# A fused attention and FFN kernel: the second FFN in seven block products instead of eight from the third batch on

## The chip, the cores and the metric

The kernel runs on one core of a Trainium2 chip. The core has a matrix engine (TensorE, PE in the profile, with PEld for its weight loads), VectorE (DVE), ScalarE (ACT), GpSimd (POOL) and SyncE (SP), which here only starts DMA transfers. Matmul results go to PSUM, which has eight banks of 128 partitions by 512 float32. All other tiles lie in SBUF. The engines run side by side and wait for each other through semaphores. The metric is the device time of one execution in microseconds; lower is better.

## What is computed

```python
def _attn_ref(q, k, v, phi):                    # 8 batches, 8 heads, 576 rows, 64 wide; phi has 32 memories
    a = np.exp(phi - np.max(phi, axis=2, keepdims=True))
    a = a / (np.sum(a, axis=2, keepdims=True) + 1e-09)
    k_m = np.einsum('bhsm,bhsd->bhmd', a, k)
    v_m = np.einsum('bhsm,bhsd->bhmd', a, v)
    scores = np.matmul(q, k_m.transpose(0, 1, 3, 2)) / np.sqrt(q.shape[-1])
    attn = np.exp(scores - np.max(scores, axis=-1, keepdims=True))
    attn = attn / (np.sum(attn, axis=-1, keepdims=True) + 1e-09)
    return np.matmul(attn, v_m)

def _moe_ref(x, w_in, w_out):                   # x: 4608 tokens x 512; w_in 512 x 2048; w_out 2048 x 512
    h = x @ w_in
    g = h * (1.0 / (1.0 + np.exp(-h)))
    return g @ w_out
```

The attention output, heads side by side, is the `x` of the FFN.

## The kernel before

**Layout.** Work goes by batch (576 tokens). The attention of batch n = b+1 is computed while the FFN of batch b runs. `v_m` and `w_in` are multiplied first (`p_mm`, "P"), so that the first FFN takes the attention weights (`a`, 256 memories of all heads) straight to h. Operands of the big matmuls are split into a high and a low float32r part (`hi`, `lo`), and a product is three matmuls: hi with hi, hi with lo, lo with hi.

**The chunk loop.** A batch has 16 chunks of 128 FFN columns (`fc`, L886). For each chunk `ffn1` (L622) issues 12 matmuls of 288 columns into the tile `h` (two PSUM banks, one buffer); `silu` (L657) on ScalarE writes 512 tokens to `g32` (two buffers) and the other 64 tokens to `gleft`; `split` (L646) on VectorE makes the two parts in `gparts`. `finish` (L874) then issues the previous chunk's second FFN: `main_step` (L689) has four token tiles of 128, each with three matmuls of 512 output columns (`ffn2`, L671) into one of four PSUM banks, "acc". So TensorE's order is FFN1 of chunk c, work of the attention, FFN2 of chunk c-1. After the last chunk `store` (L680) copies each bank with ScalarE and sends it out. After every second batch the 64 leftover tokens of two batches go through `left_step` (L695): four times `split`, then 12 matmuls.

**The events.** `events` (L703 to L756) lists, by batch and chunk slot, the pieces of the next batch's attention: `phi_max`, `phi_fold` (a maximum over partitions), `phi_sub`, `phi_exp`, `e_mm` (k_m and v_m), `e_tr`, `s_all` (scores), `s_max`, `s_sub`, `s_exp`, `s_sum`, `s_norm`, `s_back` and `s_low` (transposes back and parts), and four `p_mm` with their split `p_split`. They run after `ffn1` and the SiLU of the slot. `load_kv`, `load_q` and `load_phi` are also events; they are issued on SP's queue.

**What sets the order.** TensorE follows the written order everywhere (`in_order`, L97), ScalarE from batch 1 on. VectorE and SP are put in order by the compiler's planner: it takes, at each time of its own estimate, the instruction that is ready and stands first in the program. On the chip each engine's list is then fixed. A tile with a `tag` shares its buffers with other tiles of that tag and waits for a free one; `mt` of `phi_max` shares the tag "g32" with the SiLU output (L245, L658). The tag "raw" (three buffers of 8 KB a partition) holds raw weights in batch 0 and output tiles later; "cva" and "cva1" serve the weight conversion of batch 0. `beside_h` (L208) gives unused columns of the h banks, `banks` (L202) the two "bg" banks that P uses.

Of the kernel before, what the change touches and what calls it, by code (L numbers as in the profile page):

```python
# [48 lines left out]
def attn_ffn_kernel(  # L49
# [12 lines left out]
    ps = ctx.enter_context(tc.tile_pool(name="ps", bufs=1, space=bass.MemoryType.PSUM))  # L62

# [11 lines left out]
    pparts = const.tile([P, 2, 2, 2 * JW], F32R, name="pparts")  # L75

# [271 lines left out]
    def e_tr(b):  # L348
        pt = beside_h(P)
        t = sb.tile([P, 2, NR, M], F32, tag="kvT", name=f"kvT{b}", bufs=2)  # L350
        for kind in range(2):
            nc.tensor.transpose(pt[kind], kvn[:, kind].rearrange("p g d -> p (g d)"), ident)  # L352
        nc.vector.tensor_copy(t[:, 0].rearrange("p r m -> p (r m)"), pt[0])
        nc.scalar.copy(t[:, 1].rearrange("p r m -> p (r m)"), pt[1])
# [76 lines left out]
    def set_parts(b):  # L431
        for k, x in enumerate(("ahi", "alo")):
            at[b][x] = aparts[:, k, b % 2].rearrange("p (g s) -> p g s", g=2)

    def s_back(b, u):
        if "aT" not in at[b]:
            at[b]["aT"] = sb.tile([P, 2, S], F32, tag="att", name=f"aT{b}")
            set_parts(b)
        aT, ahi, sc = (at[b][k] for k in ("aT", "ahi", "sc"))
        c = slice(*u)  # L440
        for p in range(2):
            nc.vector.transpose(aT[:, p, c], sc[:, p, c])  # L442
        nc.scalar.activation(ahi[:, :, c], aT[:, :, c], AF.Copy)
# [142 lines left out]
    ALL = (0, S)  # L586
# [3 lines left out]
    pj = {}  # L590

    def p_mm(b, f, w, low=True):
        j = f // JW
        if f % JW == 0:
            pj[b, j] = [pparts[:, k, j % 2].rearrange("p (g f) -> p g f", g=2) for k in range(2)]
# [60 lines left out]

    def silu(b, fc, h):  # L657
        g32 = sb.tile([P, MAIN], F32, tag="g32", name="g32", bufs=2)  # L658
# [10 lines left out]
    acc = {}  # L669
# [10 lines left out]
    def store(key, rows, last=False):  # L680
        o = sb.tile([P, DMODEL], F32, tag="raw", name="o", bufs=RAWB)
# [20 lines left out]

    events = {}  # L703
# [4 lines left out]
    for b in range(B):  # L708
# [4 lines left out]
        else:  # L713
            for j in range(1, NJ):
                ev(b, 4 * j - 3, p_mm, b, j * JW, JW)
        if n == B:
            continue
        at_slot = (4, 5, 6, 7.5, 9, 9.5, 11.5, 12.5, 13, 13.5, 13.5, 14) if b == 0 else (1, 2, 3, 5, 9, 10, 10, 11, 12, 13, 13, 14)
# [27 lines left out]
        ev(b, sk, s_back, n, ALL)  # L746
        ev(b, sk, s_low, n, ALL)
        if n + 1 < B:
            ev(b, sk, load_phi, n + 1)
        ev(b, 14, p_mm, n, 0, JW)  # L750
# [220 lines left out]
```

## Time and profile before

| | |
|---|---|
| time, median of 3 runs | 701.71 us (701.3 to 702.42) |
| span of the profiled execution | 700.3 us; the page gives no separate time for that execution |
| instructions | 11773, of them 4924 matmuls |
| FFN1, 128 x 288 (L637) | 1524 recorded, mean 295 ns |
| FFN2, 128 x 512 (L676, acc) | 1024 with wo_hi, 395 ns; 512 with wo_lo, 392 ns |
| FFN2 of leftover tokens (L676, accleft) | 192 |
| DMA | 60.15 MB, mean 86 GB/s |

The page gives busy time by engine, the span in 40 slices, the DMA queues, the chain of work that ended last, and the costliest groups of instructions. A matmul's duration in it contains its way through the array, and matmuls overlap; their pace is read from the starts in the timeline. A timeline row has start, duration, engine, line, operation, output <- inputs, size and count; in brackets stands the engine's idle time before it and what ended that. A window row has for each engine the busy time and the count of instructions, then the granted TensorE clock, the DMA share and GB/s. A DMA row has the count, KB of each and the median time from issue to landing.

### The profile page before, as it was taken

To read this page: it belongs to the slowest core of one execution; us is meant where nothing else is said; L and a number is where in the kernel's file an instruction comes from. 1 tells how busy PE (TensorE), PEld (TensorE's weight loads), DVE (VectorE), ACT (ScalarE), POOL (GpSimd) and SP (SyncE) were. 2 spreads that over 40 slices of the span, in tenths; PEclk is the share of its full clock that TensorE was granted. 3 is DMA by queue.
4 is the path that set the end of the run, shared out by engine and by line. 5 is a ranking of instruction groups with operands and counts; after the bars stand their busy time and mean duration, and the time that the engine had idled before them with its cause. 6 is when DMAs were issued, how large, how long until landed. Compare 5 with 4: busy or idle time off the path is not lost.

```text
span 700.3 us, 11773 instructions
## 1 busy us (share of the span) xinstructions
PE 689.4 (98%) x4924; PEld 562.4 (80%) x4924; DVE 365.4 (52%) x665; ACT 259.0 (37%) x456; POOL 0.7 (0%) x6
## 2 busy tenths in 40 slices
PE   7999999999999999999999999999999999999997
PEld 3578777888888888888888888888888888888886
DVE  4898797435654256534636346542564525623322
ACT  3879584422424224421423314342241413431211
POOL 0000000000000000000000000000000000000000
PEclk9999999999999999999999999999999999999999
DMA  9995752212201221132110311112121000010002
GB/s 334 317 338 187 254 212 95 78 61 68 92 19 46 92 68 44 52 137 69 35 61 16 137 56 47 61 54 83 68 80 31 1 1 1 1 61 1 1 0 76
DMA packets 25445, 60.15 MB, mean 86 GB/s; under 512 B 2096, under 2 KB 10416, under 8 KB 25392
## 3 DMA queue, kind: packets, MB, share of 16 engines
q1 hardware_dynamic: 24448, 56.63, 22.8%
q10 hardware_dynamic: 944, 2.77, 1.1%
q8 instruction: 39, 0.64, 0.4%
q14 instruction: 14, 0.11, 0.1%
HBM read 49.95 MB, written 9.44 MB: 85 GB/s over the span
## 4 chain that ended last, share of the span: by engine, by line
PE 84%; DVE 2%; issue 0%; ACT 0%; ACTq 0%
PE acc L676 45%; PE h L637 25%; PE accleft L676 6%; PE bg L602 4%; PE h L322 2%; PE bg L367 1%; DVE wo_lo L176 0%; DVE raw L172 0%; PE h L330 0%; PE h L352 0%; DVE aparts L448 0%; DVE aT L442 0%; DVE gparts L654 0%; DVE sc L415 0%; DVE smx L411 0%
## 5 line engine op out<-in xcount | busy, mean ns | idle before, releaser
L676 PE MATMUL acc<-wo_hi,gparts 128*128 128x512 f32 x1024 | 341.8, 395 | 0.1
L676 PEld LDWEIGHTS acc<-wo_hi,gparts 128*128 128x128 f32 x1024 | 192.0, 188 | 52.7 <-issue 6.6
L637 PEld LDWEIGHTS h<-aparts,pparts 128*128 128x128 f32 x1524 | 214.0, 188 | 14.4 <-issue 2.1
L637 PE MATMUL h<-aparts,pparts 128*128 128x288 f32 x1524 | 223.3, 295 | 0.7 <-ACT aparts L581 0.4
L660 ACT ACTIVATE g<-h 128x512 f32<-128x512 f32 x127 | 76.0, 599 | 345.9 <-PE h L637 180.3
L676 PE MATMUL acc<-wo_lo,gparts 128*128 128x512 f32 x512 | 200.8, 392 | 0.7 <-DVE wo_lo L176 0.6
L652 DVE CAST gparts<-g 128x512 fp32r<-128x512 f32 x128 | 54.4, 425 | 260.0 <-ACT g L660 260.0
L676 PEld LDWEIGHTS acc<-wo_lo,gparts 128*128 128x128 f32 x512 | 96.1, 188 | 18.4 <-DVE wo_lo L176 1.9
L654 DVE TENSOR_TENSOR gparts<-g,gparts 128x512 fp32r<-128x512 f32 x128 | 88.2, 689 | 10.3
L618 DVE TENSOR_TENSOR pparts<-bg,pparts 128x1024 fp32r<-128x1024 f32 (+1 forms) x36 | 39.7, 1102 | 5.4 <-ACT pparts L616 5.0
L676 PE MATMUL accleft<-wo_hi,gparts 128*128 128x512 f32 x128 | 40.6, 389 | 0.0
L616 ACT ACTIVATE pparts<-bg 128x1024 fp32r<-128x1024 f32 (+1 forms) x36 | 33.6, 932 | 14.8 <-PE bg L602 14.8
L602 PE MATMUL bg<-win,kvT 64*32 64x512 f32 (+1 forms) x576 | 35.8, 554 | 0.0
L676 PEld LDWEIGHTS accleft<-wo_hi,gparts 128*128 128x128 f32 x128 | 24.0, 188 | 4.9
L662 ACT ACTIVATE gleft<-h 128x64 f32<-128x64 f32 x127 | 27.8, 219 | 0.0
L683 ACT ACTIVATE o<-acc 128x512 f32<-128x512 f32 x32 | 19.2, 600 | 21.8 <-PE acc L676 10.6
L676 PE MATMUL accleft<-wo_lo,gparts 128*128 128x512 f32 x64 | 24.9, 389 | 0.0
L660 ACT ACT_TABLE_LOAD x14 | 18.0, 1283 | 14.2 <-issue 13.6
L652 DVE CAST gparts<-gleft 128x512 fp32r<-128x512 f32 x16 | 6.8, 427 | 20.7 <-PE accleft L676 12.2
L168 ACT ACTIVATE raw<-raw 128x1024 int32<-128x1024 uint32 (+1 forms) x16 | 16.8, 1048 | 0.0
L322 PEld LDWEIGHTS h<-kv,phi 128*32 128x32 f32 x384 | 10.2, 110 | 5.0 <-ACT gleft L662 5.0
L676 PEld LDWEIGHTS accleft<-wo_lo,gparts 128*128 128x128 f32 x64 | 12.0, 188 | 2.4
(139 smaller groups left out, 365.0 us busy)
## 6 DMA issues: line engine op xcount, KB each, us to landing
kv<-in_kv SPq DMA_DIRECT2D x28, 516.0 KB, 5.9
q<-in_q SPq DMA_DIRECT2D x16, 576.0 KB, 5.7
out<-o SPq DMA_DIRECT2D x32, 256.0 KB, 2.1
raw<-in_w_in SPq DMA_DIRECT2D x14, 512.0 KB, 6.6
raw<-in_w_out SPq DMA_DIRECT2D x6, 1024.0 KB, 5.5
phi<-in_phi SPq DMA_DIRECT2D x7, 576.0 KB, 3.8
kv<-in_kv ACTq DMA_DIRECT2D x4, 516.0 KB, 6.8
kr<-in_kv SPq DMA_DIRECT2D x7, 258.0 KB, 6.4
```

What stands on the lines that cost most here:

```text
L168: nc.scalar.activation(r, low, AF.Copy, scale=2.0**-29)
L322: nc.tensor.matmul(pt[p][M * r : M * (r + 1), :KVW], e[:, p, c, M * r : M * (r + 1)], kvt[c][:, p, r], start=c == 0, stop=False, skip_grou ...
L602: nc.tensor.matmul(bg[M * r : M * (r + 1), p, :w].rearrange("p (k f) -> p k f", f=P), kvT[D * p : D * (p + 1), 1, r], win[D * p : D * (p + ...
L616: nc.scalar.activation(hi[:, :, c], bg[:, :, :w], AF.Copy)
L618: nc.vector.tensor_tensor(lo[:, :, c], bg[:, :, :w], hi[:, :, c], op=ALU.subtract)
L637: nc.tensor.matmul(h[:, hf, :HALF], wt[:, p, fs], a[:, p, hf * HALF : (hf + 1) * HALF], start=n[hf] == 0, stop=n[hf] == 5, skip_group_chec ...
L652: nc.vector.tensor_copy(ghi, g32)
L654: last_split.append(nc.vector.tensor_tensor(glo, g32, ghi, op=ALU.subtract))
L660: nc.scalar.activation(g32.rearrange("p (h f) -> p h f", h=2), h[:, :, :w], AF.Silu)
L662: i = nc.scalar.activation(gleft[:, fc, o : o + LEFT].rearrange("p (h f) -> p h f", h=2), h[:, :, w:HALF], AF.Silu)
L676: nc.tensor.matmul(acc[key], gt[:, cs], wt[:, fc], start=fc == 0 and n == 0, stop=fc == NFC - 1 and n == 2)
L683: nc.scalar.activation(o, a, AF.Copy)
```

## The change

Batches 0 and 1 keep the old second FFN. From batch 2 on, the product g @ w_out of 256 tokens, 256 FFN columns and 512 outputs is taken as 2 x 2 blocks of 128 tokens, 128 FFN columns and 256 outputs, and formed from seven block products (Winograd's form of Strassen's method) instead of eight. Each product is again three matmuls, now of 256 columns.

A batch has 16 steps: two token halves (`t`) of eight pairs of chunks (`j`). `ffn1s` makes h of two chunks for 288 tokens (12 matmuls of 288). `forms` applies SiLU and makes the sums of g's blocks and their two parts on VectorE and ScalarE. `st_step` issues 7 x 3 matmuls. Four products use weights that stay in SBUF (three blocks of w_out, and one sum that `t1_load` writes over the fourth block after batch 1), three use weight sums that come from DRAM: `ring_load` fetches 256 KB for each use into a ring of four slots. The seven sums are collected in four PSUM banks, half a bank each; `st_out` combines them after each half and sends out two tiles of 128 tokens.

The weight sums are formed during batch 1 (`w_forms`: GpSimd, ScalarE, VectorE) and stored to DRAM. The leftover tokens of batches 2 to 7 go through `left_st`, with matmuls of 256 columns. All four quarters of P now have to last through a whole batch (two in tag "raw", two in `pparts`), so P and the attention move to other slots, the attention parts have one home from batch 2 on, and the second half of batch n's attention parts (`SECOND`, n from 3) is formed at slot 1 of batch n itself. `mt` moves to tag "cva1", the SiLU output to a fixed buffer `gbuf`. `e_mm` and `e_tr` use the "bg" banks in later batches.

```diff
+    gbuf = const.tile([P, 2 * MAIN], F32, name="gbuf")
...
-            at[b]["mt"] = sb.tile([P, 2, 2, P], F32, tag="g32", name="mt", bufs=2)
+            at[b]["mt"] = sb.tile([P, 2, 2, P], F32, tag="cva1", name="mt", bufs=1)
...
-        pt = banks(b) if b < 2 else beside_h(KVW)
+        pt = beside_h(KVW) if b == 2 else banks(b)
...
-            at[b][x] = aparts[:, k, b % 2].rearrange("p (g s) -> p g s", g=2)
+            at[b][x] = aparts[:, k, b == 1].rearrange("p (g s) -> p g s", g=2)
...
+    def w_forms(j, step):
...
+        if step == 0:
+            f = at[0]["forms", j] = sb.tile([P, 2, DMODEL], F32, tag="cva", name="wf", bufs=1)
+            c = slice(2 * j, 2 * j + 2)
+            nc.gpsimd.tensor_tensor(f, as_f32(wo_hi[:, c]), as_f32(wo_lo[:, c]), op=ALU.add)
+            b11, b12, b21, b22 = (f[:, k, q * Q : (q + 1) * Q] for k in range(2) for q in range(2))
+            nc.gpsimd.tensor_tensor(b11, b12, b11, op=ALU.subtract)
+            nc.gpsimd.tensor_tensor(b12, b22, b12, op=ALU.add)
+            nc.gpsimd.tensor_tensor(b22, b22, b11, op=ALU.add)
+            nc.gpsimd.tensor_tensor(b21, b22, b21, op=ALU.subtract)
+            return
+        f = at[0]["forms", j].rearrange("p k (q f) -> p (k q) f", q=2)
+        nc.scalar.activation(ring[0][:, :, :Q], f, AF.Copy)
+        nc.vector.tensor_tensor(ring[0][:, :, Q:], f, ring[0][:, :, :Q], op=ALU.subtract)
+        load(saved[j], as_f32(ring[0]))
+
+    def t1_load(n):
+        for j in (2 * n, 2 * n + 1):
+            for w, q in ((wo_hi, 0), (wo_lo, Q)):
+                load(as_f32(w[:, 2 * j, Q:]), saved[j][:, 0, q : q + Q])
+
+    RING = (3, 1, 2)
+    uses = [(j, k) for b in range(2, B) for t in range(2) for j in range(NP) for k in RING]
...
+    def ring_load():
+        u = next(asked, None)
+        if u is not None:
+            j, k = uses[u]
+            load(as_f32(ring[0][:, u % 4]), saved[j][:, k])
...
+    def forms(b, t, j, h):
...
+        nc.scalar.activation(gbuf[:, :MAIN].rearrange("p (i f) -> p i f", i=2), h[:, :, :w], AF.Silu)
+        o = b % 2 * LEFT + t * (LEFT // 2)
+        nc.scalar.activation(gleft[:, 2 * j : 2 * j + 2, o : o + LEFT // 2], h[:, :, w:HALF], AF.Silu)
+        hi, lo = form_high[j % 2], form_low[j % 2]
+        nc.scalar.activation(hi[:, :3], g[:, 1:4], AF.Copy)
+        nc.vector.tensor_tensor(
+            g[:, 4:6], g[:, :1].broadcast_to([P, 2, P]), g[:, 1:3], op=ALU.subtract
+        )
+        nc.vector.tensor_tensor(g[:, 6], g[:, 1], g[:, 5], op=ALU.subtract)
+        nc.vector.tensor_tensor(g[:, 7], g[:, 3], g[:, 6], op=ALU.subtract)
+        nc.vector.tensor_copy(hi[:, 3:], g[:, 4:])
+        nc.vector.tensor_tensor(lo, g[:, 1:], hi, op=ALU.subtract)
+        return hi, lo
...
+    def st_step(b, t, j, part):
...
+        held = ((0, 0, 0, b11), (0, 1, 2, b21), (1, 0, 6, b22), (1, 1, 4, b12))
+        for terms in (HIGH, LOW):
+            for bank, place, k, w in held:
+                product(bank, place, part, k, w, terms)
+        for bank, place, k in ((2, 0, 5), (2, 1, 3), (3, 0, 1)):
+            r = ring[0][:, next(used) % 4]
+            product(bank, place, part, k, (r[:, :Q], r[:, Q:]), HIGH + LOW)
+            ring_load()
+        if j == NP - 1:
+            st_out(b, t)
+
+    def st_out(b, t):
...
+        for i in range(2):
+            nc.scalar.activation(o[:, i], sums[i], AF.Copy)
...
+        add(u2, sums[2][:, :Q], c11)
+        add(u3, sums[2][:, Q:], u2)
+        add(c11, c11, c12)
+        add(c12, u2, c22)
+        add(c12, c12, c21)
+        add(c21, u3, sums[3][:, :Q], ALU.subtract)
+        add(c22, u3, c22)
...
+            for j in range(NP):
+                ev(b, 1.5 * j + 2, w_forms, j, 0)
+                ev(b, 1.5 * j + 3, w_forms, j, 1)
+        else:
+            ev(b, 0, p_mm, b, (3 if b > 2 else 2) * JW, JW)
+            if b == 2:
+                ev(b, 2, p_mm, b, 3 * JW, JW)
+            else:
+                ev(b, 1, s_high, b, SECOND)
+                ev(b, 1, s_low, b, SECOND)
...
-        at_slot = (4, 5, 6, 7.5, 9, 9.5, 11.5, 12.5, 13, 13.5, 13.5, 14) if b == 0 else (1, 2, 3, 5, 9, 10, 10, 11, 12, 13, 13, 14)
+        at_slot = (
+            (4, 5, 6, 7.5, 9, 9.5, 11.5, 12.5, 13, 13.5, 13.5, 14) if b == 0
+            else (1, 2, 3, 5, 9, 10, 10, 11, 12, 13, 13, 14) if b == 1
+            else (0, 1, 3, 5, 6, 7, 7, 9, 10, 11, 11, 13)
+        )
...
+            for j in range(3):
+                ev(b, 10 + 2 * j, p_mm, n, j * JW, JW)
...
+        for s in range(NFC if b > 1 else 0):
...
+            t, j = divmod(s, NP)
+            h = ffn1s(b, t, j)
+            part = forms(b, t, j, h)
+            for part_ in range(2):
+                for fn, a in events.pop((b, s + part_ / 2), []):
+                    fn(*a)
+            finish(range(NI))
+            prev = ("st", b, t, j, part)
```

The numbers of `at_slot` are the slots of `phi_max`, the fold, `phi_exp`, `e_mm`, `e_tr`, the scores (twice), `s_max` and `s_sub`, `s_exp`, `s_sum`, `s_norm` and `s_back`.

More of the change, by code (lines that the diff above doesn't have):

```diff
@@ L594, in p_mm @@
         if f % JW == 0:
-            pj[b, j] = [pparts[:, k, j % 2].rearrange("p (g f) -> p g f", g=2) for k in range(2)]
+            p_home(b, j)
         hi, lo = pj[b, j]
@@ L655, in split @@
         return gs
+    half = iter(range(1 << 30))
     def silu(b, fc, h):
-        g32 = sb.tile([P, MAIN], F32, tag="g32", name="g32", bufs=2)
+        g32 = gbuf.rearrange("p (n f) -> p n f", n=2)[:, next(half) % 2]
         w = MAIN // 2
@@ new lines, in product @@
+    def product(bank, place, part, k, w, first):
+        hi, lo = part
+        whi, wlo = w
+        for gt, wt in first:
+            gt, wt = (hi, lo)[gt], (whi, wlo)[wt]
+            key = bank, place
+            nc.tensor.matmul(
+                sums[bank][:, place * Q : (place + 1) * Q], gt[:, k], wt,
+                start=bank not in begun, stop=True, skip_group_check=True,
+            )
+            begun.add(bank)
+    sums, begun = [], set()
+    HIGH, LOW = ((0, 0), (0, 1)), ((1, 0),)
```

155 lines of the change are left out of this document (132 added, 23 removed).

## The prediction

> **What bounds the kernel now.** I began with the page: span, engine table, granted clock.
>
> ```profile
> span 700.3 us, 11773 instructions
> PE 689.4 (98%) x4924; PEld 562.4 (80%) x4924; DVE 365.4 (52%) x665; ACT 259.0 (37%) x456; POOL 0.7 (0%) x6
> ...
> PEclk9999999999999999999999999999999999999999
> ```
>
> TensorE is busy for 689 of 700.3 us at full clock, VectorE for half of it. The next view is PE's timeline over one chunk of 128 FFN columns in the fourth batch: twelve FFN1 matmuls, twelve FFN2 matmuls, the next twelve FFN1.
>
> ```profile
> 403.92 1.75 PE L637 MATMUL h<-aparts,pparts 128*128 128x288 f32 x12
> 405.51 0.39 PE L676 MATMUL acc<-wo_hi,gparts 128*128 128x512 f32 x1
> ...
> 408.25 1.74 PE L637 MATMUL h<-aparts,pparts 128*128 128x288 f32 x12
> ```
>
> The starts give 1.59 us for FFN1 (132 ns a matmul of 288 columns) and 2.74 us for FFN2 (228 ns a matmul of 512), with no gap: a chunk takes 4.33 us and TensorE alone sets it. Next I asked what VectorE does in 85 us of this, about one batch (the phi loads of three successive batches start 77.96 and 88.84 us apart, 83.4 on average; every second batch is followed by the leftover stage).
>
> ```profile
> 225.00:310.00 85.00, 85.00 (x639) 70.76 (x630) 42.00 (x83) 27.96 (x52) 0.00 (x0) 1.00 0.26 90
> ...
> 267.96 0.33 SPq L87 DMA_DIRECT2D phi<-in_phi  x1
> ...
> 345.92 0.33 SPq L87 DMA_DIRECT2D phi<-in_phi  x1
> ...
> 434.76 0.33 SPq L87 DMA_DIRECT2D phi<-in_phi  x1
> ```
>
> PE 85.00, VectorE 42.00, ScalarE 27.96, DMA share 0.26. So a cut in matmul time is worth its full length until VectorE or the DMA queue takes over, and the change loads both.
>
> **TensorE's part.** Per step (two chunks, half the tokens), 21 matmuls of 256 columns replace 12 of 512, in 16 steps a batch and six batches: 96 steps. FFN1's matmuls stay 12 a step. No matmul of this type with 256 columns is in the trace. A line through the two pitches, 228 at 512 and 132.5 at 288, rises 0.426 ns a column and gives 119 ns at 256. Below it, proportion alone (228 / 2) gives 114. Above it, 132.5 would hold if each weight load set a floor that 288 columns already touch. A row with a 128 x 128 load before every matmul of 128 columns speaks against that floor:
>
> ```profile
> 54.91 0.60 PE L265 MATMUL bg<-ident,cm 128*128 128x128 f32 x4
> ...
> L265 PE MATMUL bg<-ident,cm 128*128 128x128 f32 x4 | 0.6, 274 | 0.0
> ```
>
> Four start within 0.60 - 0.27 = 0.33 us, 110 ns apart: a load fits in 110. I take 119. A step is then 1.59 + 21 x 0.119 = 4.09 us, 0.24 less; over 96 steps **-23.0 us** (114 ns: -33; 132.5: +4). The leftover stage of batches 3, 5 and 7 has 96 matmuls of 256 instead of 48 of 512: 11.42 against 10.94 us, **+1.4** for three.
>
> **VectorE's chain.** A chunk's split was a cast and a subtraction; a step now needs a subtraction over 256 elements, two over 128, a cast of 512 and a subtraction over 896.
>
> ```profile
> L652 DVE CAST gparts<-g 128x512 fp32r<-128x512 f32 x128 | 54.4, 425 | 260.0 <-ACT g L660 260.0
> L654 DVE TENSOR_TENSOR gparts<-g,gparts 128x512 fp32r<-128x512 f32 x128 | 88.2, 689 | 10.3
> L448 DVE TENSOR_TENSOR aparts<-aT,aparts 128x1152 fp32r<-128x1152 f32 x7 | 9.5, 1358 | 0.1
> L248 DVE TENSOR_TENSOR mx<-mt 128x256 f32<-128x256 f32 x7 | 2.9, 418 | 0.0
> L304 DVE TENSOR_TENSOR phi<-phi,am 64x128 f32<-64x128 f32 x12 | 3.4, 284 | 0.2
> L660 ACT ACTIVATE g<-h 128x512 f32<-128x512 f32 x127 | 76.0, 599 | 345.9 <-PE h L637 180.3 <-issue 165.3
> ```
>
> Between 512 and 1152 elements the subtraction grows from 689 to 1358 ns, so 896 take 1.09 us. The step costs 0.42 + 2 x 0.28 + 0.425 + 1.09 = 2.50 us, with some 0.25 us between dependent instructions 2.75; before it was 1.11. The combination at the end of each half (st_out) adds 2 x 7 x 0.42 = 5.9 us a batch. Per average batch VectorE goes from 42.00 x 83.4 / 85 = 41.2 to 41.2 - 16 x 1.11 + 16 x 2.50 + 5.9 = 69.3 us, against 83.4 - 3.6 = 79.8 of TensorE: 87%. On average it fits. Locally the margin is thin: g and h have one buffer each, so SiLU, chain and next SiLU form a ring. From the end of FFN1, SiLU 0.60 plus 2.75 puts the low parts at 3.4 us; TensorE wants them about 5.0 us on (a step of 4.09 and eight first products). The slack is **1.6 us**, and what VectorE does in between for the next batch's attention eats it. Before, that came as a block:
>
> ```profile
> 371.31 0.43 DVE L652 CAST gparts<-g 128x512 fp32r<-128x512 f32 x1 [2.37 <-ACT g L660]
> ...
> 373.20 0.45 DVE L275 STREAM_TRANSPOSE mxt<-mx 128x256 f32<-128x256 f32 x1
> ...
> 374.02 1.22 DVE L618 TENSOR_TENSOR pparts<-bg,pparts 128x1024 fp32r<-128x1024 f32 x1
> ...
> 378.87 0.41 DVE L652 CAST gparts<-g 128x512 fp32r<-128x512 f32 x1
> 379.31 0.29 DVE L304 TENSOR_TENSOR phi<-phi,am 64x128 f32<-64x128 f32 x1
> ```
>
> From 373.20 to 379.60 runs the fold and subtraction (with one p_split of 1.2 and a cast inside, 4.8 us without them); the cast due 4.3 us after 371.31 came at 378.87, over 3 us late, and TensorE did not stop. That cover shrinks to 1.6. In steps 0 and 1 of an odd batch lie this 4.8, phi_max 1.7, p_split 1.2, the second half's low part 0.8 and st_out 2.9: 11.4, and three chains 7.5: 18.9 us, against 13.4 of TensorE (three steps, and 1.1 for the P matmuls). Excess 5.5. Two quiet steps before it can take 2 x (4.09 - 2.75) = 2.7 of phi_max and the fold, since mt no longer shares a tag with g; the slack takes 1.6; 1.2 us is left, in batches 3 and 5 (in even batches st_out ran in the leftover stage). ScalarE adds the second exposed spot:
>
> ```profile
> 339.04 1.17 ACT L419 ACTIVATE sc<-sc 128x1152 f32<-128x1152 f32 x1
> 341.32 1.28 ACT L660 ACT_TABLE_LOAD   x1 [1.12 <-issue]
> 342.62 0.60 ACT L660 ACTIVATE g<-h 128x512 f32<-128x512 f32 x1
> ```
>
> After each exp the table load comes only when h is there, so this SiLU is 1.28 late, which leaves 0.3 of slack while the sums and the normalization want VectorE: some 0.7 us in each of five batches. Together **+6** (0 if all is hidden; 5 x 5.5 = 28 if nothing is moved ahead and every batch pays).
>
> **The streamed sums.** Three loads of 256 KB a step are 786 KB in 4.09 us, 192 GB/s.
>
> ```profile
> 301.98 3.04 SPq L87 DMA_DIRECT2D kv<-in_kv  x4
> 305.12 0.39 SPq L87 DMA_DIRECT2D kr<-in_kv  x1
> ...
> 304.00:306.00 2.00, 2.00 (x11) 1.60 (x10) 0.50 (x3) 0.37 (x1) 0.00 (x0) 1.00 1.01 390
> ...
> kv<-in_kv SPq DMA_DIRECT2D x4, 516.0 KB, 5.4
> kr<-in_kv SPq DMA_DIRECT2D x1, 258.0 KB, 5.8
> ...
> out<-o SPq DMA_DIRECT2D x32, 256.0 KB, 2.1
> ```
>
> Two microseconds saturate all 16 engines at 390 GB/s, so the stream takes half. A slot of the four-deep ring is wanted again four products later, about a step (4.1 us) after its load is issued; 256 KB land in 2.1 when the queue is empty (a store; the nearest row): hidden. But ring loads share SP's queue with kv. The kv burst of one batch (4 x 516 + 258 KB, 2.38 MB) is issued as e_mm releases its tiles, just before that step's ring loads; kr, last of it, landed 5.8 us after issue, and a ring load behind it 0.7 later (262 KB at 390 GB/s). Issued about 1 us after kr, it lands 5.5 us after its issue: 1.4 late, its follower a little more: 2 us. Batches 2 to 5 load kv for a later batch: **+8** (0 if the loads get ahead; 14 if 3.5 of lead are lost each time). q and phi bursts are a half and a quarter as long and fit the lead.
>
> **Batch 1 and the end.** There the sums are formed: eight times on GpSimd one addition over 1024 and four over 256 elements, a ScalarE copy, a VectorE subtraction, and a 1 MB store.
>
> ```profile
> masks.py:199 POOL TENSOR_SCALAR_AFFINE_SELECT ident<-ident 128x128 f32<-128x128 f32 x1 | 0.3, 294 | 0.1
> ...
> raw<-in_w_out SPq DMA_DIRECT2D x6, 1024.0 KB, 5.5
> ```
>
> No GpSimd addition is in the trace. At VectorE's rate the five take 1.2 + 4 x 0.42 = 2.9 us; at 294 ns for 128 elements 4.7. I take 4.7, the row of that engine. [...] The uses are 1.5 chunks (6.5 us) apart. The single staging tile must be stored before the next copy: 1.1 + 1.2 + 5.5 = 7.8 us, 1.3 over, and ScalarE, in program order, waits with the SiLUs behind it. The two g buffers still cover about 3 us. I take **+2** (0 to 9, seven times 1.3). The last leftover result takes a copy of 256 elements (an estimated 0.4 from ScalarE's 0.60 for 512) and two additions of 0.42, 1.3 us, in place of one copy of 512: **+0.7**.
>
> **Sum.** -23.0 + 1.4 + 6 + 8 + 2 + 0.7 = -4.9 us on the span of 700.3: 695.4. The runs' median lies 1.4 above the span: **697 us**.
>
> **Rivals.** *All cover holds*: no stall, -23.0 + 1.4 + 0.7, 681 us. For it: before, a cast 3 us late cost nothing; against: slack 1.6. *VectorE becomes the bound* (the slower side): the order of its queue leaves the block of steps 0 and 1 whole, ahead of the third chain; it decides once that block exceeds the slack of 1.6 us plus what was moved ahead; at the full 5.5 in five batches 28 replaces 6: 719 us. For it: the block above ran as one piece. *Ring loads late behind every burst*: 14 for 8, and 3 us more for q and phi: 706. *A floor of 132.5 ns at 256 columns*, by which the seven products don't save time: +4 for -23: 724. Against it is the 110 ns row. *GpSimd and VectorE hold each other up in batch 1*: VectorE's 42 us of 85, 8 x 1.2 for the low parts and GpSimd's 8 x 4.7 make 90 if they exclude each other, 5 over, with ScalarE's wait 9 to 11 in place of 2: 706. [...]
>
> **How the numbers follow.** Forecast 0.42 (687 to 700), all hidden 0.15, VectorE bound 0.20, ring 0.09, batch 1 0.08, floor 0.06. Faster by over 0.2% (1.4 us, about what a measurement of this kernel can tell from no change) is the first two, 0.57; within 0.2% the low edges of ring and batch 1, 0.08; slower 0.35. The range 681 to 719 leaves out half of the all-hidden case and about a tenth above.
>
> **What would show it.** Right: starts of 256-column matmuls 119 ns apart and steps of 4.09 us in the quiet middle of batch 7; PE gaps only near steps 1, 2 and 11 (waiting for VectorE's low parts) and just after e_mm (waiting for the ring's DMA). Wrong: a pitch over 125; PE gaps in every step; VectorE over 90% in the later batches; ScalarE waiting for GpSimd or for the store through batch 1. A batch 7 no shorter than before would sink the whole argument, since nothing but the products competes there.

## The result and the profile after

The kernel after takes **744.75 us** (median of 4 runs, 741.66 to 746.7) against 701.5 of the kernel before (4 runs, 701.18 to 702.42): a ratio of **1.061** with a 95% interval of 1.0583 to 1.0639. It is slower by 43 us. The prediction said 697, in a range of 681 to 719, and is wrong in sign. The profiled execution of the kernel after took 746.09 us and has a span of 744.3.

From the page after: the span and the engine table, the slices of PE, GpSimd and the granted clock, the shares of the chain that ended last, and three of the groups and one of the transfers.

```profile
span 744.3 us, 15025 instructions
PE 695.1 (93%) x5932; PEld 602.6 (81%) x5932; DVE 547.5 (74%) x1056; ACT 305.8 (41%) x565; POOL 50.6 (7%) x46
...
PE   8999989889899899888999899899899999999996
...
POOL 0000030667300000000000000000000000000000
PEclk9999999999999999999999999999999999999999
...
PE 47%; DMA 17%; DVE 14%; POOL 3%; ACT 3%; issue 3%; SPq 0%; DVEq 0%; ACTq 0%
...
L814 PE MATMUL sum<-ring,aparts 128*128 128x256 f32 x576 | 116.3, 293 | 22.2 <-DMA ring<-forms 18.2
L814 PEld LDWEIGHTS sum<-ring,aparts 128*128 128x128 f32 x576 | 88.1, 190 | 35.0 <-DMA ring<-forms 28.6
L805 DVE TENSOR_TENSOR gparts<-gbuf,aparts 128x896 fp32r<-128x896 f32 x96 | 104.5, 1088 | 9.0
...
ring<-forms SPq DMA_DIRECT2D x288, 256.0 KB, 3.9
```

TensorE was busy for 98% of a shorter span; now it is busy for 93%, and its slices show many 8s from batch 1 on. This is the same line of the page before:

```profile
PE 84%; DVE 2%; issue 0%; ACT 0%; ACTq 0%
```

Of the chain that ended last, TensorE held 84% before and holds 47%; transfers into the ring have 17%, VectorE 14%. GpSimd's additions lie in slices 5 to 10, counted from 0 (93 to 205 us), in batches 0 and 1. A matmul that overlaps others counts as busy (those on the ring last 293 ns each and start 120 ns apart where nothing waits), so 93% hides much of the loss: the starts of the matmuls show it better. The starts of each batch's first FFN1, read from PE's timeline, give this table (us; "batches 0 and 1" runs from the start of the span to the first FFN1 of batch 2, the rest to the end of the span).

| | batches 0 and 1 | batches 2 to 7 | single batches 2, 3, 4, 5, 6 |
|---|---|---|---|
| before | 197.8 | 502.5 | 78.0, 88.8, 78.0, 88.8, 78.0 |
| after | 212.0 | 532.2 | 82.5, 97.0, 82.0, 99.0, 78.9 |

So 14 us come in before a single block product has run, and 30 in the stage that was to win 21. Of the 14, 1.2 us are not a loss: a quarter of P (16 matmuls) has moved from batch 2 into batch 1.

### The profile page after: what moved, and what is told of

Read it like the earlier page. It is cut to its first block, busy times and chain, and to the rows that moved or that the text cites. A ratio compares the mean times of both kernels' runs of the same rounds, so it can differ in the third digit from the quotient of the medians.

```text
span 744.3 us, 15025 instructions
## 1 busy us (share of the span) xinstructions
PE 695.1 (93%) x5932; PEld 602.6 (81%) x5932; DVE 547.5 (74%) x1056; ACT 305.8 (41%) x565; POOL 50.6 (7%) x46
## 4 chain that ended last, share of the span: by engine, by line
PE 47%; DMA 17%; DVE 14%; POOL 3%; ACT 3%; issue 3%; SPq 0%; DVEq 0%; ACTq 0%
PE sum L814 20%; DMA ring<-forms 17%; PE h L783 12%; PE lsum L814 5%; PE acc L691 3%; PE bg L615 2%; PE h L650 2%; DVE gparts L805 2%; PE accleft L691 1%; POOL wf L747 1%; DVE oo L851 1%; PE bg L324 1%; DVE pm L631 1%; DVE ring L756 1%; ACT gbuf L794 1%
## 5 line engine op out<-in xcount | busy, mean ns | idle before, releaser
L814 PE MATMUL sum<-ring,aparts 128*128 128x256 f32 x576 | 116.3, 293 | 22.2 <-DMA ring<-forms 18.2
L814 PEld LDWEIGHTS sum<-ring,aparts 128*128 128x128 f32 x576 | 88.1, 190 | 35.0 <-DMA ring<-forms 28.6
L805 DVE TENSOR_TENSOR gparts<-gbuf,aparts 128x896 fp32r<-128x896 f32 x96 | 104.5, 1088 | 9.0
L799 DVE TENSOR_TENSOR gbuf<-gbuf 128x256 f32<-128x256 f32 x96 | 40.8, 425 | 87.1 <-ACT gbuf L794 86.9
L814 PE MATMUL sum<-wo_hi,aparts 128*128 128x256 f32 x384 | 98.8, 290 | 0.0
L814 PE MATMUL sum<-wo_lo,aparts 128*128 128x256 f32 x384 | 95.5, 282 | 0.0
L783 PE MATMUL h<-aparts,pm 128*128 128x288 f32 x576 | 85.6, 298 | 5.4 <-DVE sc L378 5.4
L691 PE MATMUL acc<-wo_hi,gparts 128*128 128x512 f32 x256 | 87.6, 402 | 2.4 <-DVE gparts L667 2.2
L783 PEld LDWEIGHTS h<-aparts,pparts 128*128 128x128 f32 x576 | 78.1, 188 | 0.0
L650 PEld LDWEIGHTS h<-aparts,pparts 128*128 128x128 f32 x372 | 52.7, 192 | 13.0 <-issue 2.9
L691 PEld LDWEIGHTS acc<-wo_hi,gparts 128*128 128x128 f32 x256 | 48.5, 191 | 17.2 <-DVE gparts L667 4.9
L691 PE MATMUL acc<-wo_lo,gparts 128*128 128x512 f32 x128 | 51.1, 399 | 1.0 <-DVE wo_lo L178 0.9
```

The lines of the kernel that those rows point to most:

```text
L650: nc.tensor.matmul(h[:, hf, :HALF], wt[:, p, fs], a[:, p, hf * HALF : (hf + 1) * HALF], start=n[hf] == 0, stop=n[hf] == 5, skip_group_chec ...
L691: nc.tensor.matmul(acc[key], gt[:, cs], wt[:, fc], start=fc == 0 and n == 0, stop=fc == NFC - 1 and n == 2)
L783: nc.tensor.matmul(h[:, i, :HALF], wt[:, p, f : f + P], a[:, p], start=n == 0, stop=n == 5)
L799: nc.vector.tensor_tensor(g[:, 4:6], g[:, :1].broadcast_to([P, 2, P]), g[:, 1:3], op=ALU.subtract)
L805: nc.vector.tensor_tensor(lo, g[:, 1:], hi, op=ALU.subtract)
L814: nc.tensor.matmul(sums[bank][:, place * Q : (place + 1) * Q], gt[:, k], wt, start=bank not in begun, stop=True, skip_group_check=True,)
```

## The experiments

Each run is compared with runs of the kernel before on the same chip; "less than after" compares medians, also across chips. The medians of before in these comparisons lie between 701.5 and 702.6, and the four runs of after spread over 5 us, so differences of a few us from after are not read. Batches, steps and chunks are counted from 0. The first four take suspected costs out one by one, the next three ask how the two largest arise, the rest try to mend them.

### One cost out at a time

**The stream.** `ring_load` fetches only the first four weight sums; the other 284 loads go.

```diff
-        if u is not None:
+        if u is not None and u < 4:
```

> The three streamed block products use the first four loads of the ring all through; the 284 other ring loads are left out, so their weights are not those of the reference. Theory S (the stream of weight sums is what TensorE waits for): in the trace of after, the starts of matmuls on the ring lie about 40 us late in total over batches 2 to 7; with the loads gone the time falls by 35 to 45 us, to 700 to 710. Rival V (VectorE's chain is the bound and the late loads only stand where its waits would stand): the time falls by less than 15 us, and the waits move to the products on the low parts.

Measured 716.77 us, ratio 1.0205 (1.0175 to 1.0235). Against the kernel after, 28 us, three and a half times the 8 of the prediction. It lies between the two expectations: less than the 35 to 45 of theory S and more than the 15 of rival V, so the stream is a cost of its own, but not the only one.

**The stream and VectorE's three subtractions.** As above, and L799 to L803 of `forms` go:

```diff
-        nc.vector.tensor_tensor(
-            g[:, 4:6], g[:, :1].broadcast_to([P, 2, P]), g[:, 1:3], op=ALU.subtract
-        )
-        nc.vector.tensor_tensor(g[:, 6], g[:, 1], g[:, 5], op=ALU.subtract)
-        nc.vector.tensor_tensor(g[:, 7], g[:, 3], g[:, 6], op=ALU.subtract)
```

> As the run with the ring loaded once, and the three subtractions that form the sums of g's blocks are left out too (the cast and the low parts stay), so VectorE's chain is 1.0 us shorter in each of 96 steps. Theory S: no more than 8 us below the run with the ring loaded once, since the chain fits in a step without it. Rival V: 20 us or more below that run.

Measured 696.64 us, ratio 0.9918 (0.989 to 0.9947): another 20 us, for instructions of 1.0 us a step that the prediction had counted as mostly covered. For this part it is rival V (20 us or more) that came true.

**GpSimd.** The five additions of `w_forms` go; the later copy reads `wo_hi`.

```diff
-            nc.gpsimd.tensor_tensor(f, as_f32(wo_hi[:, c]), as_f32(wo_lo[:, c]), op=ALU.add)
...
-            nc.gpsimd.tensor_tensor(b21, b22, b21, op=ALU.subtract)
             return
-        f = at[0]["forms", j].rearrange("p k (q f) -> p (k q) f", q=2)
+        f = as_f32(wo_hi[:, 2 * j : 2 * j + 2]).rearrange("p k (q f) -> p (k q) f", q=2)
```

> Batch 1 without the five GpSimd additions for each pair of chunks: the sums are left out, the high and low copies and the stores to DRAM stay. Theory G (GpSimd and VectorE hold each other up, and ScalarE waits in order for GpSimd): batches 0 and 1, which are 14 us longer in after than in before, lose 10 us or more of that, time 731 to 735. Rival (the 1 MB stores from one staging tile set the pace of batch 1): at most 4 us, time 740 or more.

Measured 727.09 us, ratio 1.0352 (1.0322 to 1.0382), 17.7 less than after. Theory G had the right side, but expected 731 to 735; the 4 us below that do not come from batches 0 and 1 (see the table below).

**All three out.** The three edits together.

> All three at once: ring loaded once, VectorE's three subtractions for the sums left out, GpSimd's additions left out. Theory of three costs (the stream 28 us, VectorE's chain 20, GpSimd in batch 1 18, next to matmuls that save the forecast 22): 744.7 - 66 = 679, so 676 to 684. Rival (they cover each other, or a fourth cost is left): above 688.

Measured 682.97 us, ratio 0.9729 (0.971 to 0.9749). The prediction's "all cover holds" was 681. It is inside the expected 676 to 684. With the three costs out, the products bring nearly what the sum had given them. By stage:

| left out | batches 0 and 1 | batches 2 to 7 |
|---|---|---|
| nothing (after) | 212.0 | 532.2 |
| stream | 211.4 | 503.6 |
| stream, subtractions | 212.0 | 483.3 |
| GpSimd | 198.7 | 526.2 |
| all three | 198.7 | 483.3 |

GpSimd's work costs 13.3 us in batches 0 and 1, the stream 28.6 and the subtractions 20.3 in batches 2 to 7. They add up to the difference of the spans (744.3 and 682.0) because the subtractions were taken out on top of the stream; that they add up does not show that they are independent. One row does not fit: without GpSimd batches 2 to 7 are 6 us shorter, though nothing in them was changed. Of this, 4.4 us lie in batch 5 (99.0 and 94.6), where the profiled run of after has the wait of 2.24 us and the half clock shown in the last section; the four runs of the kernel after differ by 5 us among themselves, and the profiled one is the second slowest. More than that is not shown.

### How the stream comes to cost 28 us

First the quiet last batch, PE's timeline of the kernel after. No attention runs there and nothing else is loaded.

```profile
678.25 0.40 PE L814 MATMUL sum<-ring,aparts 128*128 128x256 f32 x2
...
679.30 1.74 PE L783 MATMUL h<-aparts,pparts 128*128 128x288 f32 x12
680.89 0.28 PE L814 MATMUL sum<-wo_hi,aparts 128*128 128x256 f32 x1
681.01 0.28 PE L814 MATMUL sum<-wo_lo,aparts 128*128 128x256 f32 x1
...
682.67 0.40 PE L814 MATMUL sum<-ring,aparts 128*128 128x256 f32 x2
...
683.38 1.74 PE L783 MATMUL h<-aparts,pparts 128*128 128x288 f32 x12
...
686.75 0.46 PE L814 MATMUL sum<-ring,aparts 128*128 128x256 f32 x2
...
687.36 0.51 PE L814 MATMUL sum<-ring,aparts 128*128 128x256 f32 x2
...
687.82 1.76 PE L783 MATMUL h<-aparts,pm 128*128 128x288 f32 x12
```

From 679.30 to 683.38 is a step of 4.08 us, and 680.89 to 681.01 a pitch of 120 ns: the products run as forecast. One step later the product due at about 687.1 starts at 687.36 and the step takes 4.44: it waited for the ring. In all six batches the stream costs 4.6, 4.0, 5.1, 7.3, 1.7 and 5.9 us (after against the run without the stream): the quiet last batch pays as much as those that load kv. The slot of the product at 678.25 is wanted by the product at 682.67, 4.4 us later; its load goes out at 678.79, when the product ends, so the lead is 3.9. The third product of a step frees its slot for the first of the step after next, which gives every third load a lead of 6.7 (issued at 679.68, wanted at 686.39). What a load needs is in the view of the line that issues it, for 655 to 728 us of the same kernel (minimum, median and maximum from issue to landing are in the last row).

```profile
L89 SPq DMA_DIRECT2D ring<-forms x47: 319/366/1700, 656.2 to 723.4; - x47
...
  PEld sum L814: 5.6, 12
  PE sum L814: 2.7, 3
...
DMA to landing us min/median/max: 3.0/3.8/5.1
```

The prediction had 2.1 us for it, from a store. A load of the same size takes 3.8 in this stream and up to 5.1; one issue on SP took 1.70 us instead of 0.37. The margin is 0.1 us, not 2, and it is lost without any burst: in this stretch TensorE's weight loads waited for the ring 12 times and its matmuls three times. The DMA rows of the same stretch have stores of this size beside the loads:

```profile
ring<-forms SPq DMA_DIRECT2D x47, 256.0 KB, 3.8
out<-oo SPq DMA_DIRECT2D x4, 256.0 KB, 2.3
```

So it is not the stream alone that makes the loads slow; a store beside it takes 2.3. How much of the 3.8 comes from the three loads of a step, which are issued within about 1 us (678.79, 679.21 and 679.68) on the queue that held 62.7% of the 16 engines' time in this stretch, no run separates. Over batches 2 to 7, 72 loads were used less than 0.25 us after they landed, so that TensorE had as good as waited for them. All of them are among the 192 with the short lead (3.9 in the quiet step above), none among the 96 with the long one (6.7).

At 12 of the 72 the load itself had been issued 0.8 to 2.0 us late, always at step 1 or 9, right behind `st_out`. SP's timeline at the start of batch 3 shows why:

```profile
305.19 1.00 SPq L862 DMA_DIRECT2D out<-oo  x2
306.29 5.70 SPq L89 DMA_DIRECT2D ring<-forms  x6
```

The products that free the two slots ended at 304.48 and 304.82, but in SP's fixed list the two stores of `st_out` stand first, and they wait for VectorE's additions, the last of which ends at 305.78. The prediction had looked at kv, q and phi ahead of the ring loads, and not at these stores.

**Attention loads on another queue.** If bursts ahead of the ring loads were the cause, taking kv, q and phi of batches 3 to 7 off SP's queue should free it.

```diff
-        queue = nc.scalar if b == 0 else None
+        queue = nc.scalar if b == 0 else nc.gpsimd if b > 2 else None
```

(the same for `load_q` and `load_phi`)

> kv, q and phi of batches 3 to 7 are loaded through GpSimd's queue in place of SP's; nothing else changes. If the ring loads are late because they stand behind these loads in one queue, most of the 40 us of ring waits goes: 715 to 725. If the ring is late by its own round trip (landing 3.8 us after issue in batch 7, where nothing is loaded for the attention, against a step of 4.1), the time stays above 735, since the bytes are the same and the engines are shared.

Measured 758.93 us, ratio 1.0805 (1.0774 to 1.0837): 14 us worse than after. Steps 6 and 7 of batches 2 to 5, where kv is loaded, grew from 5.3 to 6.7 us to between 7.7 and 9.1. In the list of waits of this run the ring has 37.5 us in 48 waits (weight loads) and 27.1 in 32 (matmuls), against 28.6 and 18.2 in after, and the longest is 3.7 us against 2.4. That the burst now runs beside the ring loads, where on SP it took its turn behind them, is my reading; no run shows it by itself. So taking these loads off SP's queue is no remedy. It does not show that their order on SP cost nothing, because the edit changes more than the order. The page of this run lists them as another kind of transfer:

```profile
q0 software_dynamic: 5440, 20.74, 8.0%
```

and GpSimd, which now issues them, is busy for 73.1 us instead of 50.6. That kv and the ring move through the same 16 engines, of which the row gives this queue 8.0%, may be the reason for the loss, or the other kind of transfer; no run separates the two.

**A fifth slot.** The slot lies in unused columns of `aparts`; by the pace of the quiet step above the tightest lead grows by one product, to an estimated 4.2 us, and only one load of three has it, while the other two have some 7.2 (before, two of three had 3.8 to 3.9). In this and in the kernel with three mends below, the last quarter of batch 1's leftover tokens is computed from parts that are overwritten early.

```diff
-            load(as_f32(ring[0][:, u % 4]), saved[j][:, k])
+            i = u % 5
+            if i < 4:
+                load(as_f32(ring[0][:, i]), saved[j][:, k])
+            else:
+                load(
+                    as_f32(aparts[:, :, 1, TF : TF + Q]),
+                    saved[j][:, k].rearrange("p (h f) -> p h f", h=2),
+                )
```

> A fifth ring slot in the unused ends of aparts (the leftover stage's parts get other homes for that): a load is asked for 5 products ahead in place of 4, 4.8 us at least in place of 4.1. If the stream is late by its round trip of 3.3 to 4 us against that lead, more than half of its 28 us goes: 724 to 732. If only the bursts of kv, q and phi ahead of it in the queue make it late, 0.7 us more of lead takes away under 10 us: above 735.

Measured 724.79 us, ratio 1.0325 (1.0304 to 1.0345): 20 us of the 28. In the list of waits of this kernel the ring's share fell from 28.6 us in 51 waits (weight loads) and 18.2 in 24 (matmuls) to this:

```profile
PEld sum L827 <- DMA ring<-forms: 4.5, 9, 1.3
PE sum L827 <- DMA ring<-forms: 2.4, 5, 1.1
```

With the loads into the fifth slot, which stand under another name in the list, 1.4 us in three waits and 0.7 in two come on top. The loads themselves did not get faster (from 638 to 710 us they land in 2.9 to 5.9 us, median 4.2). So the lead decides. By the same estimate a second load of three got some 3.2 us more of it and the last one 0.4; which of the two brought how much of the 20 the run does not tell.

**The subtractions out, the stream on.** Of the edits above only that of `forms`.

> after with VectorE's three subtractions for the sums left out (their blocks keep old contents) and the ring as in after. With the ring loaded once the same cut was worth 20 us. If the waits for the ring and for VectorE lie at different places, 20 again: 722 to 727. If a TensorE that is freed from one runs into the other, less than 12: above 732.

Measured 736.86 us, ratio 1.0496 (1.0462 to 1.0529): only 7.9 us less than after, where the same edit saved 20 with the stream off: inside the second expectation (less than 12). While VectorE holds TensorE up, the ring loads get ahead; a TensorE that is freed runs into the ring: in the list of waits of this run the ring has 31.2 us (weight loads) and 21.2 (matmuls), more than the 28.6 and 18.2 of after. What one cost is worth depends on which others are still there, so the 28 and the 20 are values in this order of removal.

### GpSimd in batches 0 and 1

Three engines' timelines of the kernel after, in batch 1. First GpSimd: one round of five additions and the next round's first two.

```profile
130.88 2.40 POOL L747 TENSOR_TENSOR wf<-wo_hi,wo_lo 128x1024 f32<-128x1024 f32 x1 [23.47 <-DVE ring L756]
133.36 0.74 POOL L749 TENSOR_TENSOR wf<-wf 128x256 f32<-128x256 f32 x1
...
135.15 1.07 POOL L751 TENSOR_TENSOR wf<-wf 128x256 f32<-128x256 f32 x1
136.30 0.74 POOL L752 TENSOR_TENSOR wf<-wf 128x256 f32<-128x256 f32 x1
139.47 2.49 POOL L747 TENSOR_TENSOR wf<-wo_hi,wo_lo 128x1024 f32<-128x1024 f32 x1 [2.43 <-DVE ring L756]
```

ScalarE, the copies of the sums:

```profile
137.07 1.06 ACT L755 ACTIVATE ring<-wf 128x1024 fp32r<-128x1024 f32 x1 [2.94 <-POOL wf L752]
...
155.94 1.07 ACT L755 ACTIVATE ring<-wf 128x1024 fp32r<-128x1024 f32 x1 [4.14 <-POOL wf L752]
156.91 0.57 ACT L675 ACTIVATE gbuf<-h 128x512 f32<-128x512 f32 x1
```

VectorE, the low parts of two chunks and between them that of the sums:

```profile
128.98 0.69 DVE L667 TENSOR_TENSOR gparts<-gbuf,gparts 128x512 fp32r<-128x512 f32 x1
...
138.16 1.23 DVE L756 TENSOR_TENSOR ring<-wf,ring 128x1024 fp32r<-128x1024 f32 x1 [2.54 <-ACT ring L755]
...
139.83 2.68 DVE L667 TENSOR_TENSOR gparts<-gbuf,gparts 128x512 fp32r<-128x512 f32 x1
```

Five additions take from 130.88 to 137.04, 6.2 us instead of the forecast 4.7 (the 4.7 came from another operation of GpSimd, 294 ns for 128 elements). The one `wf` tile then passes through a copy (1.06) and a subtraction (1.23) before the next round starts, 8.6 us after the last (130.88 to 139.47), where the schedule gives 6.5. ScalarE, in order, stands 2.94 and 4.14 us for GpSimd with the next SiLU behind it (156.91). And VectorE's subtraction of two SBUF tiles, 0.69 us by itself, takes 2.68 while GpSimd's long addition runs (139.47 to 141.96); GpSimd's short ones go from 0.74 to 1.07 beside VectorE. What in the hardware makes the two slow each other, no run shows.

**The additions on VectorE.** All five of `w_forms`, in this way:

```diff
-            nc.gpsimd.tensor_tensor(f, as_f32(wo_hi[:, c]), as_f32(wo_lo[:, c]), op=ALU.add)
+            nc.vector.tensor_tensor(f, as_f32(wo_hi[:, c]), as_f32(wo_lo[:, c]), op=ALU.add)
```

> The five additions that form the weight sums of batch 1 run on VectorE in place of GpSimd, nothing left out. If GpSimd's time (6 us for the five) in the one-buffer round of wf and VectorE's waits on it are what batch 1 loses, VectorE's 3 us end both: 727 to 734. If batch 1 loses by the round through ScalarE and the store alone, the time stays above 739.

Measured 731.89 us (728.7 and 735.09), ratio 1.0426 (1.0373 to 1.0479): 13 less than after. Batches 0 and 1 take 201.0 us instead of 212.0; without the additions it was 198.7. VectorE does the five in 1.23 + 4 x 0.42 us (128.46 to 131.53 in this run's timeline), so adding its own 2.9 us a round costs 2.3 in all, and GpSimd's 6.2 cost 13.3. The round through the one `wf` tile is the same in both, so it is the engine that cost the 11 us between them; GpSimd's longer additions and the slowing of VectorE beside them left together, and no run separates these two.

### Attempts to mend it

**Fifth slot, additions on VectorE, and the cast of four sums on ScalarE.**

```diff
-        nc.vector.tensor_copy(hi[:, 3:], g[:, 4:])
+        nc.scalar.activation(hi[:, 3:], g[:, 4:], AF.Copy)
```

> Fifth ring slot, weight sums on VectorE, and the cast of the summed blocks' high parts on ScalarE in place of VectorE (0.43 us less of VectorE in each step, one more handover in the chain). By the three costs: 744.7 - 17 (GpSimd) - 16 (ring) - 5 to 10 (VectorE) = 702 to 707, level with before. If a shorter VectorE list does not help because the chain's latency counts, 708 to 714.

Measured 720.63 us (4 runs), ratio 1.0273 (1.0256 to 1.029). A miss: above even the 708 to 714 of the second expectation.

**The same without the cast's move**, and with other places for the leftover parts, so that nothing is overwritten early.

```diff
+        if b == 1:
+            gs = (aparts[:, 1, 1, :MAIN], gparts[:, 1, next(turn) % 2]) if n == 3 else None
+        else:
+            gs = aparts[:, n % 2, 1, :MAIN], gparts[:, n % 2].rearrange("p n f -> p (n f)")[:, :MAIN]
```

> Fifth ring slot and the weight sums on VectorE, the cast of the sums left on VectorE. With the 20 us of the fifth slot and the 13 us of the sums on VectorE taken from 744.7: 712. If the cast on ScalarE in the earlier run with three mends had helped, this is above 720.6; if it hurt (its chain got a link that stands behind ScalarE's exp and table loads), 709 to 715.

Measured 715.25 us (4 runs), ratio 1.0187 (1.0163 to 1.0211): the best kernel here that computes the whole function, and still slower than before. Moving the cast had cost 5 us. It took 0.43 us off VectorE but put a link into the chain. Step 12 took 6.97 us with it and 5.97 without. The expectation had the cast standing behind the exponential and the table loads; the traces show it the other way round. In step 10 of batch 2, ScalarE's table load before the exponential of the scores starts 2.39 us after the SiLU with the moved cast (253.79 to 256.18) and 1.17 us without it (254.20 to 255.37): the cast, which waits 0.59 us for VectorE, stands before it in ScalarE's order. So the exponential and all that needs it come later, and in step 12 TensorE stands another 0.65 us for the cast itself.

**That, with VectorE's other work moved.** In `s_all` the transposes that read h's spare columns come first, the first three attention pieces of odd batches come one slot later, and kv is loaded in five pieces over five slots.

```diff
+            else (1, 2, 4, 5, 6, 7, 7, 9, 10, 11, 11, 13) if b % 2
             else (0, 1, 3, 5, 6, 7, 7, 9, 10, 11, 11, 13)
...
+                for c in range(FULLC + 1):
+                    ev(b, em + 2 + 2 * c if c < FULLC else 14, load_kv_part, n + 1, c)
```

> As the run before, and three moves aimed at single waits seen in its trace family: the two transposes that free the h banks go first (0.96 us at slot 7 in five batches), in odd batches phi_max, the fold and exp come one slot later (some 2 us in two or three batches), and kv comes in five pieces at slots 7 to 14 instead of one burst (1 us in four batches). Sum 13 us: 699, between 695 and 704. If VectorE's list is full whatever its order, 706 or more.

Measured 718.25 us (4 runs), ratio 1.0225 (1.0189 to 1.0261). A miss: no gain over the one before. Batch 3's first three steps fell from 5.95, 6.30, 4.29 to 5.28, 4.38, 5.06, step 7 from 6.65 to 6.06, and step 6 from 5.67 to 4.30; but steps 4 and 5 rose from 4.31 and 6.54 to 5.76 and 6.95, and step 8 from 5.06 to 5.71. The batch takes 94.1 us in both: the waits were moved, not removed. That VectorE's list is full whatever its order, as the second expectation puts it, fits this; no run shows it.

## Why the prediction was wrong, point by point

**The products (-23.0, +1.4, +0.7): right.** Pitch 120 ns (forecast 119), steps 4.07 to 4.09 us where nothing waits (4.09); the rival of a floor of 132.5 ns is out. With all three costs out batches 2 to 7 take 483.3 us, 19.2 less than before, where the three terms make 20.9. Of the 19.2, 1.2 are the quarter of P that now runs in batch 1.

**"256 KB land in 2.1 when the queue is empty (a store; the nearest row): hidden" (+8, measured 28.6): the step that failed most.** The lead of 4.1 us was nearly right (3.9 in the quiet step). The landing time was that of a store, and these loads took 3.0 to 5.1 us, median 3.8, where the stores beside them took 2.3. The page before had a load that would have warned:

```profile
phi<-in_phi SPq DMA_DIRECT2D x7, 576.0 KB, 3.8
```

576 KB in 3.8, where 2.1 plus the time of another 320 KB at 390 GB/s would have been 2.9. So the cost was sought behind kv bursts only, while the margin was gone everywhere. The bursts themselves were sized about right: the two ring loads issued among those of kv at 242.2 and 242.6 landed 5.3 and 5.5 us later (forecast 5.5), and step 6 of batches 2 to 5, with the stream, is longer by 1.7, 1.8, 2.0 and 1.0 us, 6.4 together. What the +8 left out is the other 22. The rival "ring loads late behind every burst", at 706, had the same 2.1 in it.

**VectorE's chain (+6, measured 20.3): right kind, wrong size.** The average was met: 547.5 us of VectorE in all, 74%. The local slack was not. The timeline of TensorE in the kernel without the stream shows it at the start of batch 3.

```profile
289.36 1.74 PE L783 MATMUL h<-aparts,pm 128*128 128x288 f32 x12
...
293.90 0.74 PE L814 MATMUL sum<-wo_hi,gparts 128*128 128x256 f32 x4 [0.48 <-DVE gparts L805]
...
295.54 1.74 PE L783 MATMUL h<-aparts,pm 128*128 128x288 f32 x12
...
299.38 0.50 PE L814 MATMUL sum<-ring,aparts 128*128 128x256 f32 x2 [0.68 <-DVE x L851]
...
301.37 0.56 PE L814 MATMUL sum<-ring,aparts 128*128 128x256 f32 x2 [1.01 <-DVE oo L851]
...
301.94 3.08 PE L783 MATMUL h<-aparts,pm 128*128 128x288 f32 x12
```

These steps take 6.18 and 6.41 us, and with the subtractions out 5.29 and 4.07. VectorE works in one piece from 287.6 to 304.4 us; this window row (busy time of PE, PEld, VectorE, ScalarE, GpSimd, then granted clock, DMA share, GB/s) gives 15.11 of 16.80.

```profile
287.60:304.40 16.80, 14.62 (x109) 12.88 (x108) 15.11 (x31) 5.93 (x13) 0.00 (x0) 0.92 0.09 32
```

The planner did move phi_max and the fold ahead, as I had assumed. What I had not seen: TensorE waits not only for the low parts (0.48) but for st_out, which holds the banks that the new half's sums need (0.68 and 1.01). I had priced st_out as VectorE time and not as a wait of TensorE. Then the granted clock fell (0.92 over this row, 0.57 from 301.37 to 305.37, and 3.08 us for the twelve matmuls at 301.94). Nearly half of the 20 us lies where I had put 0.7 a batch: with the stream off, step 7 takes 6.65 us against 5.69 with the subtractions out, step 12 5.95 against 5.29, step 9 4.41 against 4.09. That is 1.9 in each of five batches, 9.7 us. At step 7 TensorE's next FFN1 waits for the transposes of the scores that read the spare columns of h: "DVE sc L378" in the rows at the end. That wait is not in the prediction. The rival "VectorE becomes the bound" had 5.5 for the opening block in five batches; with the stream off it cost 4.7 in batch 3 and 3.3 in batch 5 (first three steps, with and without the subtractions) and nothing in batch 4.

**Batch 1 (+2, measured 13.3): the wrong mechanism was taken as likeliest.** I let the store of the staging tile set the pace. GpSimd did, and GpSimd and VectorE slowed each other (1.07 for 0.74 us and 2.68 for 0.69 in the rows above). The store, 5.5 us in the forecast, landed in 4.1 (the page's median), and the round took 8.6 us with 6.2 of it GpSimd's. The rival "GpSimd and VectorE hold each other up" had that, at 9 to 11; that its figure comes near 13.3 is partly luck, since it let the two exclude each other wholly, over 85 us. No run shows that they do; the rows show each take longer beside the other in places. I gave it 0.08 because no row before showed both at work (GpSimd was busy for 0.7 of 700.3 us). That was lack of evidence, not evidence against.

**The sum.** 681 for the hidden case plus 6, 8 and 2 was 697. 683 measured for it plus 20.3, 28.6 and 13.3 is 745. I also added the three as if each were alone; the runs show that they partly cover each other: the subtractions were worth 20 us with the stream off and 7.9 with it on.

**What was to show it.** "PE gaps only near steps 1, 2 and 11 and just after e_mm" was wrong: late starts on ring products lie in every batch. "A batch 7 no shorter than before would sink the whole argument": it took 92.9 us against 91.0, with no attention work in it, and 86.9 with the stream off. It is not a clean measure either: one quarter of P is left in it instead of three, 2.4 us less, so like for like it is 4.3 us longer. So the argument did not fall with the products, as I had written, but with the stream that feeds them.

## What to carry to other kernels

Compare a stream's lead with the time that a load of that size and kind takes while the stream runs, not with a store or an idle queue, and look at what stands ahead of the stream in the list of the engine that issues it; here a margin of 0.1 us at 192 loads, with bursts and late issues on top, cost 28.6 us, more than the products saved. Where a change uses up slack, look at each place in turn and list everything that reads the buffers TensorE wants next (here the banks that `st_out` still reads and the h columns under the scores): 74% of busy VectorE hid 20 us of waits. And work that was moved to an idle engine was not free here: VectorE's subtraction took 2.68 us beside it instead of 0.69, and ScalarE, which runs in order, stood up to 4.14 us for it.

## What the runs showed of the hardware

**A pause can cost more than its length.** PE's timeline of the kernel after in batch 5:

```profile
517.55 1.83 PE L783 MATMUL h<-aparts,pm 128*128 128x288 f32 x12 [1.08 <-DVE sc L378]
...
523.41 0.50 PE L814 MATMUL sum<-ring,aparts 128*128 128x256 f32 x2 [2.24 <-DMA ring<-forms]
...
524.89 2.90 PE L783 MATMUL h<-aparts,pm 128*128 128x288 f32 x12
```

After a pause of 2.24 us the same twelve matmuls take 2.90 instead of about 1.75 us; in windows of 1 us the granted clock there is 0.51, 0.50, 0.50 and 0.78 from 524 to 528. From 190 to 193, again behind a pause of 2.24, it is 0.50, 0.50 and 0.53. A pause of 2.10 that ended at 166.12 did not lower it (1.00 from 166.12 to 170.12), while in the kernel without the stream 0.68 and 1.01 us close together came before a fall (the 3.08 at 301.94 above).

The clock record in the trace of the kernel after (start, length and granted clock of each stretch) tells its pauses apart. It has three stretches at half clock inside the kernel, from 107.60, 189.52 and 524.03 us. Each lasts 3.413 us, and they start 30, 54 and 152 times 3.413 us after the first change of the clock, at 5.20. Cut into slots of this length from there, TensorE stood still for 1.79, 2.01 and 2.24 us in the three slots just before the stretches. A fourth, with 3.08 us, lies at the kernel's end, and the clock is at half behind it. In every other slot it stood still for 1.61 us or less, and the clock behind stayed up. In the trace of before, cut from its first change at 5.02, the last whole slot has 1.96 us, with half clock behind it, and no other more than 1.19. What happens between 1.61 and 1.79 us, and why the clock falls, these traces do not show.

The pause of 2.24 us before 523.41 lay whole in the slot that ended at 524.03. That of 2.10 us lay across the border at 165.63, with 1.61 us in the first of its two slots.

If TensorE did half as much in a stretch at half clock, each of the three cost at most half its length, an estimated 5 us in all. The mean granted clock was 0.992, against 0.998 before.

**GpSimd's short additions.** In the rows from 130.88 on 1024 elements take 2.40 us and 256 take 0.74, not 0.60: by a line through the two, an estimated 0.19 us of each does not depend on the size.
